# Reading K, V and wq in 64 KB pieces, each written to two neighbouring partitions

## The chip, the cores and the metric

The kernel runs on one core of one Trainium2 chip. The metric is device time in microseconds (us); lower is better. Times are medians of several runs. Runs of each kernel within 0.3% count as undisturbed ("fast"). Where a ratio of two kernels is given, it is the mean time of the one kernel's fast runs over the mean of the other's fast runs of the same rounds, so it is not quite the ratio of the medians that stand beside it.

## The reference

One decoding step of a transformer layer for a single token: layer norm, grouped-query attention against a cache of 65,536 keys for each of 8 key/value heads, then a gated feed-forward block. Shortened to what matters (not word for word):

```python
def _A_ref(x, k_cache, v_cache, wq, wo):          # x is the normed token
    q = (x @ wq)                                   # 32 heads of 128
    k = jnp.repeat(k_cache, 4, axis=1)             # k_cache, v_cache: (1, 8, 65536, 128) bf16
    v = jnp.repeat(v_cache, 4, axis=1)
    scores = jnp.einsum("bhqd,bhkd->bhqk", q, k) * (Dh ** -0.5)
    p = _softmax(scores, axis=-1)
    o = jnp.einsum("bhqk,bhkd->bhqd", p, v)
    return o.transpose(...).reshape(B, Sq, Hq * Dh) @ wo
```

K and V are 134 MB each. Every byte is used once, so the kernel has to bring 282 MB into the on-chip memory (SBUF, in 128 partitions), and that decides its time: in the profile below the DMA row is at 9 in 39 of 40 slices, while PE, the busiest compute engine, is busy 60% of the span.

## The kernel before

The keys of a head are cut into 4 blocks of 16,384 keys. A block of K or V is 4 MB: partition p takes 128 consecutive keys, which are 32 KB in one piece, in memory and in the partition. Four slots of 32 KB a partition form a ring; a load waits until the slot's last user is done. All large loads are issued by SP (SyncE), in the order wq, K0 to K3, then K and V in turn.

```python
SLOT = T * DH                                  # 128 keys x 128: 32 KB a partition
ring = sb("ring", [128, NSLOT * SLOT], bf16)   # NSLOT = 4
...
order = [("wq", 0)]
order += [("K", b) for b in range(NR)]
for b in range(NR, NB):
    order += [("K", b), ("V", b - NR)]
order += [("V", NB - 4), ("V", NB - 3), ("V", NB - 2), ("V", NB - 1), ("wg", 0), ("wu", 0), ("wd", 0)]
...
        if k == "wq":
            dma("sp", lambda e, d=dst: e.dma_start(d.rearrange("p (k n) -> p k n", k=4),
                A_wq.rearrange("(p k) n -> p k n", p=128)), f"r{s}", deps, "wq")
...
            src = cache[0, h, r * BLK:(r + 1) * BLK, :].rearrange("(p t) d -> p (t d)", t=T)
            if ld == ("V", NB - 1):
                ...                            # the last V block goes in two parts
            else:
                dma("sp", lambda e, d=dst, sr=src: e.dma_start(d, sr), f"r{s}", deps, f"{k}{b}")
```

For each K block the vector engine (DVE) transposes 8 chunks, the matrix engine (PE) makes the scores, and four blocks later PE multiplies with V. ACT and POOL in the profiles are the scalar engine and GpSimd.

Of the kernel before, what the change touches and what calls it, by code (L numbers as in the profile page):

```python
# [9 lines left out]
ALU = mybir.AluOpType  # L10
# [12 lines left out]
NSLOT = 4  # L23
# [3 lines left out]
WH = 4 * WJ  # L27
PO_BANKS = (5, 6)
MISC = 7


class Prog:
# [10 lines left out]
    def op(self, eng, fn, deps=(), name=None):  # L43
        assert name is None or name not in self.where, name
        self.ops[eng].append(dict(fn=fn, deps=[d for d in deps if d], name=name, dma=None))
        if name:
            self.where[name] = (eng, len(self.ops[eng]) - 1)

    def dma(self, eng, fn, sem, deps=(), name=None):
        self.op(eng, fn, deps, name)  # L50
        rec = self.dma_sems.setdefault(sem, dict(sem=None, count=0))
        rec["count"] += 16
        self.ops[eng][-1]["dma"] = (sem, rec["count"])
# [43 lines left out]
def bass_sequential_preLN__gqa_block_cached__glu_gated_glu__decode_kernel(  # L97
# [10 lines left out]
    SLOT = T * DH  # L108
# [7 lines left out]
    with ExitStack() as es:  # L116
        def sb(name, shape, dt):
            return es.enter_context(nc.sbuf_tensor(name, shape, dt))

        ring = sb("ring", [128, NSLOT * SLOT], bf16)  # L120
# [52 lines left out]
        def ps(bank, c0, c1, p0=0, p1=128):  # L173
            return PS[p0:p1, bank * 512 + c0: bank * 512 + c1]

        def psap(bank, c0, dims, p0=0, np_=128):
            return bass.AP(tensor=PS, offset=p0 * 4096 + bank * 512 + c0, ap=[[4096, np_]] + dims)

        def slot_ap(s):
            return ring[:, s * SLOT:(s + 1) * SLOT]  # L180

        P = Prog(nc, es)
        op, dma = P.op, P.dma
# [12 lines left out]
        def freed(ld):  # L196
            if ld is None:
                return None
            k, b = ld
            return {"wq": "q", "K": f"T{b}.{NC - 1}", "V": f"PV{b}"}[k]  # L200

        dma("act", lambda e: e.dma_start(x_row[:, :], A_x[0]), "x", name="x")
        V_SPLIT = [(0, 6), (6, 8)]
        for ld in order:
            k, b = ld
            s = slot_of[ld]
            dst = slot_ap(s)
            deps = [freed(prev[ld])]
            if k == "wq":
                dma("sp", lambda e, d=dst: e.dma_start(d.rearrange("p (k n) -> p k n", k=4),  # L210
                    A_wq.rearrange("(p k) n -> p k n", p=128)), f"r{s}", deps, "wq")
            elif k in ("wg", "wu"):
                w = B_w_gate if k == "wg" else B_w_up
                dma("sp", lambda e, d=dst, w=w: e.dma_start(d[:, 0:4 * FF].rearrange("p (k n) -> p k n", k=4),
                    w.rearrange("(p k) n -> p k n", p=128)), f"r{s}", deps, k)
            elif k == "wd":
                src = B_w_down.rearrange("(p r) n -> p r n", p=128)
                for i, (r0, r1) in enumerate(WD_SPLIT):
                    dma("sp", lambda e, d2=dst[:, r0 * D:r1 * D].rearrange("p (r n) -> p r n", n=D), sr=src[:, r0:r1, :]:
                        e.dma_start(d2, sr), f"wd{i}", deps if i == 0 else (), f"wd{i}")  # L220
            else:
                h, r = b // NR, b % NR
                cache = A_k_cache if k == "K" else A_v_cache
                src = cache[0, h, r * BLK:(r + 1) * BLK, :].rearrange("(p t) d -> p (t d)", t=T)
                if ld == ("V", NB - 1):
                    for i, (c0, c1) in enumerate(V_SPLIT):
                        dma("sp", lambda e, d=dst, sr=src, a=c0 * CH, z=c1 * CH: e.dma_start(d[:, a:z], sr[:, a:z]),
                            f"vl{i}", deps if i == 0 else (), f"V{b}.{i}")
                else:
                    dma("sp", lambda e, d=dst, sr=src: e.dma_start(d, sr), f"r{s}", deps, f"{k}{b}")  # L230
            if ld == ("V", NB - 4):
                for i, (j0, nj, nr) in enumerate(WO):
                    src = A_wo[j0 * DH:(j0 + nj) * DH, :]
                    dst = ktw[:, j0 * D:(j0 + nj) * D]
                    if nr:
                        src = src.rearrange("(p r) n -> p (r n)", r=nr)
                    else:
                        src, dst = src.rearrange("(j p) n -> p j n", p=128), dst.rearrange("p (j n) -> p j n", j=nj)
                    dma("sp", lambda e, src=src, dst=dst: e.dma_start(dst, src), f"wo{i}",  # L239
                        [f"S{NB - 1}"] if i == 0 else (), f"wo{i}")  # L240
# [26 lines left out]
        def ln_stats(i, src_dep, bank, c0):  # L267

            op("dve", lambda e: e.tensor_copy(hT[i][:, :], ps(*src_dep[1])), [src_dep[0]], f"hT.{i}")
            op("dve", lambda e: e.tensor_tensor(sq[:, :], hT[i][:, :], hT[i][:, :], ALU.mult), [f"hT.{i}"], f"sq.{i}")  # L270
            op("dve", lambda e: e.tensor_reduce(st[i][:, 0:1], hT[i][:, :], AX.X, ALU.add), (), f"sta.{i}")
            op("dve", lambda e: e.tensor_reduce(st[i][:, 1:2], sq[:, :], AX.X, ALU.add), [f"sq.{i}"], f"st.{i}")
            op("pe", lambda e: e.matmul(ps(bank, c0, c0 + 2), lhsT=onesf[:, :], rhs=st[i][:, :], start=True, stop=True),
               [f"st.{i}", f"sta.{i}", "onesf"], f"tot.{i}")
# [13 lines left out]
        for kt in range(4):  # L288
            lhsT = bass.AP(tensor=x_row, offset=kt, ap=[[D, 1], [4, 128]])
            op("pe", lambda e, lhsT=lhsT, kt=kt: e.matmul(ps(MISC, kt, kt + 1), lhsT=lhsT, rhs=ident[0:1, 0:1], start=True, stop=True,  # L290
                                                          skip_group_check=True),
               ["x", "ident"] if kt == 0 else (), "xTp" if kt == 3 else None)
        for b in PO_BANKS:
            op("pe", lambda e, b=b: e.matmul(ps(b, 0, 512), lhsT=zrow[0:1, 0:128], rhs=zrow[0:1, :], start=True, stop=True),
               ["zrow"], f"z{b}")
        ln_stats(0, ("xTp", (MISC, 0, 4)), 0, 0)
        op("dve", lambda e: e.tensor_copy(xT[:, :], hT[0][:, :]), ["hT.0"], "xT")
# [17 lines left out]
        for je in range(4):  # L315
            src = qh[:, je * 128:(je + 1) * 128]
# [3 lines left out]
        for i in range(4):  # L320
            dst = bass.AP(tensor=ktw, offset=32 * i * KTW_ROW + W0 + i * 32 + NC - 1,
                          ap=[[KTW_ROW, 32], [WH, HKV], [WJ, 4], [NC, 4]])
            src = psap(2, 0, [[4, HKV], [32, 4], [1, 4]], 32 * i, 32)
# [38 lines left out]
        def softmax(h):  # L362
# [3 lines left out]
               [f"mx{NR * h + r}" for r in range(NR)], f"gm{h}")  # L366
            op("pe", lambda e: e.matmul(ps(MISC, 0, 128, 0, 1), lhsT=gm[:, k:k + 1], rhs=identf[:, :], start=True, stop=True),  # L367
               [f"gm{h}", "identf", "xT", f"ls{h - 1}" if h else None], f"gmT{h}")
            op("dve", lambda e: e.tensor_reduce(gmj[:, 4 * k:4 * k + 4], ps(MISC, 0, 128, 0, 1).rearrange("p (i a c) -> p a i c", a=4, c=NC),
                                                AX.XY, ALU.max), [f"gmT{h}"], f"gmj{h}")  # L370
            op("dve", lambda e: e.tensor_copy(gmrep[:, :].rearrange("p (i a c) -> p i a c", a=4, c=NC),  # L371
                                              bass.AP(tensor=gmj, offset=4 * k, ap=[[8, 1], [0, 4], [1, 4], [0, NC]])),
               [f"gmj{h}"], f"gmrep{h}")
            op("pe", lambda e: e.matmul(ps(MISC, 128, 129), lhsT=gmrep[0:1, :], rhs=one_f[0:1, 0:1], start=True, stop=True),  # L374
               [f"gmrep{h}", "onef"], f"neg{h}")
            op("act", lambda e: e.activation(negmax[:, k:k + 1], ps(MISC, 128, 129), AF.Copy, scale=-att_scale),  # L376
               [f"neg{h}", f"E{NR * h - 5}" if h >= 2 else None], f"negmax{h}")
# [115 lines left out]
        for i, (nm, bank) in enumerate((("wg", GB), ("wu", UB))):  # L493
# [7 lines left out]
            if i == 0:  # L501
                for g in range(4):
                    for kt in range(4):
                        dst = psap(YB, kt, [[4, 32]], 32 * g, 1)
                        op("pe", lambda e, g=g, kt=kt, dst=dst: e.matmul(
                            dst, lhsT=hT[1][:, kt:kt + 1], rhs=identf[:, 32 * g:32 * g + 32],
# [53 lines left out]
```

## Time and profile before

| | before |
|---|---|
| time, median of 4 runs | 667.54 us (667.23 to 667.81) |
| bytes from memory | 282.33 MB |
| PE, DVE, ACT busy | 60%, 54%, 5% |
| first data packet begins | 1.76 us after the first instruction |
| last load has landed | 662.5 us |

The head of the page of before: busy times, then the span in 40 slices. In the DMA row a 9 means that the 16 DMA engines were at least 90% busy in that slice; GB/s is what they moved.

```profile
span 665.9 us, 5728 instructions
## 1 busy us (share of the span) xinstructions
PE 396.3 (60%) x2545; PEld 162.8 (24%) x2545; DVE 359.2 (54%) x408; ACT 34.1 (5%) x90; POOL 8.5 (1%) x12
...
DMA  9999999999999999999999999999999999999996
GB/s 378 440 433 417 439 436 425 428 439 428 423 440 433 423 435 433 430 427 438 429 427 436 430 430 429 432 433 429 435 425 436 429 426 439 430 429 409 427 426 249
DMA packets 11586, 282.70 MB, mean 425 GB/s; under 512 B 1193, under 2 KB 2218, under 8 KB 2602
```

```profile
start us, us, engine line op out<-in xcount [idle before <-releaser]
0.74 0.39 SPq L210 DMA_DIRECT2D ring<-in_A_wq_dram  x1
```

### The profile page before, as it was taken

What the parts mean: (1) busy time and instruction counts of PE and PEld (TensorE: products, weight loads), DVE (VectorE), ACT (ScalarE), POOL (GpSimd) and SP (SyncE); (2) the same over time, 40 slices, a digit from 0 to 9 for tenths busy, and PEclk for the clock granted to TensorE, in tenths of its full rate; (3) what the DMA queues carried; (4) which work ended last, traced back from release to release, by engine and by line L of the source; (5) the groups of instructions that cost most, each with busy time, mean ns of one, the idle gap of its engine ahead of it and who ended that gap; (6) DMA issues with size and microseconds to landing.
All of it is one profiled execution on the core that took longest, in us unless ns stands there. A gap on an engine that the chain in (4) does not pass through costs nothing.

```text
span 665.9 us, 5728 instructions
## 1 busy us (share of the span) xinstructions
PE 396.3 (60%) x2545; PEld 162.8 (24%) x2545; DVE 359.2 (54%) x408; ACT 34.1 (5%) x90; POOL 8.5 (1%) x12
## 2 busy tenths in 40 slices
PE   3778586565458664555665644666554567655344
PEld 2522232222123221222222212222221222223212
DVE  6579865574447655464555744476544645553002
ACT  0200100020002000020000200010000200002000
POOL 4000000000000000000000000000000000000000
PEclk9789798677787866788876778887677987768566
DMA  9999999999999999999999999999999999999996
GB/s 378 440 433 417 439 436 425 428 439 428 423 440 433 423 435 433 430 427 438 429 427 436 430 430 429 432 433 429 435 425 436 429 426 439 430 429 409 427 426 249
DMA packets 11586, 282.70 MB, mean 425 GB/s; under 512 B 1193, under 2 KB 2218, under 8 KB 2602
## 3 DMA queue, kind: packets, MB, share of 16 engines
q1 hardware_dynamic: 11560, 282.33, 98.9%
q8 instruction: 20, 0.33, 0.2%
q14 instruction: 4, 0.03, 0.0%
q10 hardware_dynamic: 2, 0.00, 0.0%
HBM read 282.33 MB, written 0.00 MB: 424 GB/s over the span
## 4 chain that ended last, share of the span: by engine, by line
DMA 67%; DVE 22%; PE 9%; ACT 1%; issue 0%; SPq 0%
DMA ring<-in_A_k_cache_dram 58%; DVE ktw L342 21%; PE PS L356 6%; DMA ring<-in_A_v_cache_dram 4%; DMA ring<-in_B_w_up_dram 4%; DMA ring<-in_A_wq_dram 2%; PE PS L307 1%; PE PS L419 1%; DVE M_sb L343 1%; ACT ktw L324 0%; DVE PT_sb L388 0%; PE PS L521 0%; PE PS L497 0%; SPq L239 0%; DVE hh L513 0%
## 5 line engine op out<-in xcount | busy, mean ns | idle before, releaser
L356 PE MATMUL PS<-ktw 128*128 128x512 bf16 x1024 | 294.1, 449 | 201.3 <-DVE ktw L342 196.1
L342 DVE STREAM_TRANSPOSE ktw<-ring 128x1024 f32<-128x1024 f32 x256 | 292.1, 1207 | 180.9 <-DMA ring<-in_A_k_cache_dram 180.9
L356 PEld LDWEIGHTS PS<-ktw 128*128 128x128 bf16 x1024 | 107.4, 110 | 384.6 <-DVE ktw L342 243.7
L419 PE MATMUL PS<-ring,PT_sb 128*16 128x512 bf16 x1024 | 70.6, 424 | 21.1 <-DMA ring<-in_A_v_cache_dram 21.1
L343 DVE TENSOR_REDUCE M_sb<-PS 128x1 f32<-128x512 f32 x32 | 22.1, 692 | 49.9 <-PE PS L356 49.9
L419 PEld LDWEIGHTS PS<-ring,PT_sb 128*16 128x16 bf16 x1024 | 28.4, 113 | 53.8 <-DMA ring<-in_A_v_cache_dram 25.3
L376 ACT ACTIVATE negmax<-PS 128x1 f32<-128x1 f32 x8 | 1.4, 171 | 550.2 <-PE PS L374 550.2
L388 DVE STREAM_TRANSPOSE PT_sb<-P_sb 128x512 bf16<-128x512 bf16 x32 | 21.8, 711 | 11.9 <-ACT P_sb L385 11.9
L433 DVE CAST O<-PS 128x4 bf16<-128x4 f32 x8 | 1.3, 162 | 39.1 <-PE PS L430 39.1
L385 ACT ACTIVATE P_sb<-PS,negmax 128x512 bf16<-128x512 f32 x32 | 21.6, 685 | 0.3
L307 PE MATMUL PS<-ring,xz 128*32 128x128 bf16 x128 | 9.7, 253 | 3.0 <-DMA ring<-in_A_wq_dram 3.0
L307 PEld LDWEIGHTS PS<-ring,xz 128*32 128x32 bf16 x128 | 9.6, 116 | 3.0 <-issue 3.0
L284 POOL TENSOR_TENSOR rstd<-ve,nhalf 128x1 f32<-128x1 f32 x2 | 1.1, 554 | 645.6 <-DVE ve L282 645.6
L430 PE MATMUL PS<-sel_bf,po_sb 128*128 128x4 bf16 x32 | 2.0, 168 | 11.4 <-ACT po_sb L427 11.4
L427 ACT ACTIVATE po_sb<-PS,rl 128x512 bf16<-128x512 f32 x8 | 5.5, 693 | 45.1 <-PE PS L419 45.1
L367 PE MATMUL PS<-identf,gm 128*1 128x128 f32 x16 | 3.0, 271 | 7.8 <-DVE gm L365 7.8
L385 ACT ACTIVATION_READ_ACCUMULATOR P_sb<-PS,negmax 128x1 f32 x32 | 6.5, 202 | 0.0
L456 PE MATMUL PS<-O,ktw 128*128 128x1 bf16 x128 | 4.9, 173 | 2.6 <-DMA ktw<-in_A_wo_dram 2.4
L257 DVE TENSOR_SCALAR rows_i<-rows_i 128x128 int32<-128x128 int32 x1 | 6.1, 6101 | 0.0
L259 DVE TENSOR_SCALAR cols_i<-cols_i 128x128 int32<-128x128 int32 x1 | 6.0, 6028 | 0.0
L374 PE MATMUL PS<-one_f,gmrep 1*128 1x1 f32 x16 | 3.0, 256 | 4.9 <-DVE gmrep L371 4.9
L456 PEld LDWEIGHTS PS<-O,ktw 128*128 128x128 bf16 x128 | 4.6, 118 | 2.9 <-DMA ktw<-in_A_wo_dram 2.2
(72 smaller groups left out, 56.8 us busy)
## 6 DMA issues: line engine op xcount, KB each, us to landing
ring<-in_A_k_cache_dram SPq DMA_DIRECT2D x32, 4096.0 KB, 29.7
ring<-in_A_v_cache_dram SPq DMA_DIRECT2D x31, 4096.0 KB, 35.6
ring<-in_A_wq_dram SPq DMA_DIRECT2D x1, 4096.0 KB, 12.1
ring<-in_A_v_cache_dram SPq DMA_DIRECT2D x1, 3072.0 KB, 32.6
ktw<-in_A_wo_dram SPq DMA_DIRECT2D x1, 2048.0 KB, 14.7
ktw<-in_A_wo_dram SPq DMA_DIRECT2D x2, 1024.0 KB, 18.1
ring<-in_B_w_gate_dram SPq DMA_DIRECT2D x1, 1792.0 KB, 38.5
ring<-in_B_w_up_dram SPq DMA_DIRECT2D x1, 1792.0 KB, 24.6
```

Of the source, the lines that this page charges most:

```text
L257: op("dve", lambda e: e.tensor_scalar(rows_i[:, :], rows_i[:, :], 3, 3, op0=ALU.arith_shift_right, op1=ALU.bitwise_and), ["rows"], "rows2")
L259: op("dve", lambda e: e.tensor_scalar(cols_i[:, :], cols_i[:, :], 3, None, op0=ALU.bitwise_and), ["cols"], "cols2")
L307: op("pe", lambda e, kt=kt, n=n, last=last: e.matmul(ps(1, 0, 128, 0, 32), lhsT=xz[:, kt * 63 + 31 - n: kt * 63 + 63 - n], rhs=wq_v[:, kt, ...
L342: op("dve", lambda e, d=dst, sr=src: e.transpose(d, sr), deps, f"T{b}.{c}")
L343: op("dve", lambda e: e.tensor_reduce(M_sb[:, b % 8:b % 8 + 1], ps(b % NS, 0, 512), AX.X, ALU.max), [f"S{b}"], f"mx{b}")
L356: op("pe", lambda e, n=n, je=je, c=c: e.matmul(ps(b % NS, 0, 512), lhsT=w_ap(h, je, c), rhs=kt_ap(n, je), start=(c == 0 and je == 0), stop ...
L367: op("pe", lambda e: e.matmul(ps(MISC, 0, 128, 0, 1), lhsT=gm[:, k:k + 1], rhs=identf[:, :], start=True, stop=True), [f"gm{h}", "identf", ...
L385: op("act", lambda e, b=b: e.activation(P_sb[:, (b % 4) * 512:(b % 4 + 1) * 512], ps(b % NS, 0, 512), AF.Exp, bias=negmax[:, k:k + 1], sca ...
L388: op("dve", lambda e, b=b: e.transpose(PT_sb[:, (b % 8) * 512:(b % 8 + 1) * 512], P_sb[:, (b % 4) * 512:(b % 4 + 1) * 512]), [f"E{b}", f"P ...
L419: op("pe", lambda e, lhsT=lhsT, tq=tq, t0=t0, c=c: e.matmul(ps(bank, 0, 512, 32 * tq, 32 * tq + 16), lhsT=lhsT, rhs=ring[:, s * SLOT + t0 ...
L427: op("act", lambda e: e.activation(po_sb[:, :], ps(PO_BANKS[k], 0, 512), AF.Copy, scale=rl[:, k:k + 1]), [f"PV{NR * h + NR - 1}", f"rl{h}" ...
L456: op("pe", lambda e, lhsT=lhsT, r=r, nt=nt, end=end: e.matmul(ps(YT, nt, nt + 1), lhsT=lhsT, rhs=src[:, r:r + 1], start=False, stop=end, s ...
```

## The change

The intent: the reads are twice as long and half as many, so whatever each read costs besides its bytes is paid half as often. Two neighbouring partitions hold 64 KB that lie together in memory, so one read can feed both. For this the changed kernel adds the copy as a bare instruction with 64 source rows of 64 KB and a separate destination pattern (partition step 1 twice, then step 2, 64 times).

```diff
+SB_PART = 1 << 18
...
+        def load_wide(e, col, src, n, w):
+            row = NSLOT * SLOT
+            wide = bass.AP(tensor=src.tensor, offset=src.offset, ap=[[w * n, 128 // w], [1, w * n]])
+            return e.add_instruction(mybir.InstDMACopy(
+                name=nc.get_next_instruction_name(), engine=mybir.EngineType.SP, queue="qSPDynamicHW", mode="Copy",
+                cce_op=ALU.bypass, ins=e.lower_ap_dma(wide), outs=e.lower_ap_dma(ring[:, col:col + n]),
+                dst_dge_shape=(SB_PART, w, w * SB_PART, 128 // w, 0, 1, 0, 1),
+                bass_dst_dge_shape=((w * row, 128 // w), (row, w), (1, n))))
...
-                dma("sp", lambda e, d=dst: e.dma_start(d.rearrange("p (k n) -> p k n", k=4),
-                    A_wq.rearrange("(p k) n -> p k n", p=128)), f"r{s}", deps, "wq")
+                dma("sp", lambda e, s=s: load_wide(e, s * SLOT, A_wq, SLOT, 2), f"r{s}", deps, "wq")
...
-                    dma("sp", lambda e, d=dst, sr=src: e.dma_start(d, sr), f"r{s}", deps, f"{k}{b}")
+                    dma("sp", lambda e, s=s, sr=src: load_wide(e, s * SLOT, sr, SLOT, 2), f"r{s}", deps, f"{k}{b}")
```

The last V block, wo and the feed-forward weights are loaded as before.

## The prediction

> **What bounds it now.** The page's slice table has the DMA row at 9 (90% or more) in 39 of 40 slices, nearly all at 423 to 440 GB/s, while PE is 60% busy, DVE 54%, ACT 5%. Taking the trace's packet records one by one, all 16 DMA engines have a packet in flight without a gap from about 12.7 us to the last weight landing at about 658 us. The chain of waits agrees: from 95 to 589 us it only alternates between K landings (57.6% of the span) and the DVE transposes that they release. So the span is (bytes / DMA rate) plus about 20 us, before the data flows and after the last landing, that the change does not touch.
>
> **The packets.** In the records a packet takes almost exactly bytes / 27.2 GB/s plus a constant: 7,168 B takes 272 ns (263.5 + 8.5), 16,384 B 611 to 615, 32,768 B 1213 at the 5th percentile, 1216 at the median, 1220 in the mean (1204.7 + 8 to 15). 16 x 27.2 is 435 GB/s[...]. So 32 KB packets already run at 432 of 435 GB/s.
>
> **What the change does.** Bytes, destinations, order of issue, semaphores and waits stay; 64 loads (wq, 32 K, 31 V) change from 128 rows of 32 KB to 64 rows of 64 KB with two writes each. Per DMA engine that is 512 reads now and 256 then. If the constant (8.5 ns) is paid per read, 256 x 8.5 = 2.2 us go; if the stalls above it (15 ns in the mean) halve as well, 3.9 us; if it is paid per write, nothing. All of it is on the critical path, because the stream is continuous. The bound, no cost per packet at all, is 512 x 15 = 7.7 us (1.2%), so a gain over 2% is practically excluded.
>
> **The danger** is which engine writes which partition. [...] The diff does not tell how rows are dealt out; I give this a little less than one chance in four.
>
> **Prediction.** 665.9 us (667.7 less 1.8), 80% range 663.3 to 671. Faster by over 2%: 0.03; within 2%: 0.75; slower: 0.22.
>
> **What would show each step.** About 7,500 packets in all instead of 11,586, the 64 KB ones of about 2418 ns (2409.4 + 8.5); if the records stay 32 KB of 1213 ns, the constant belongs to the write and the gain is nil. The DMA row stays 9; issue to landing about 29.6 us for K. DVE and PE busy times unchanged, the first landing (wq, 12.1 us) within 0.2 us.
>
> **What would make it wrong.** [...] 64 KB packets clearly over 2.5 us, or uneven between engines, and under 400 GB/s per slice; then K landings lengthen and everything follows. [...] Or a gain over 4 us, which would mean that part of the 1204.7 ns itself is no rate limit.

The 27.2 GB/s in the prediction is the slope of the packet records of before: 32,768 B take 1213 ns and 7,168 B take 272 ns, so 941 ns for 25,600 B; about 8.5 ns of either packet are left over, and 435 GB/s is 16 times that slope. The sum came to 667.7 - 1.8 = 665.9 us. The "slower: 0.22" and the upper end of the range are the author's guess.

## More of the kernel before

No compute engine is busy for more than 60% of the span (PE); the DMA engines are 90% busy or more in every slice but the last. The stretch from 100 to 590 us shows it without the ends (after the stretch: its length, busy time of each engine, granted clock, DMA share, GB/s):

```profile
core 0: us, PE busy (x) PEld busy (x) DVE busy (x) ACT busy (x) POOL busy (x), PEclk, DMA share, GB/s
100.00:590.00 490.00, 288.39 (x1660) 113.57 (x1660) 269.03 (x286) 21.44 (x60) 0.00 (x0) 0.78 1.00 431
```

The share is 1.00: a packet is in flight on every DMA engine all the time.

The issue of the loads, by tile on the SP queue (duration in ns: least, median, most), and the first load in the timeline:

```profile
L230 SPq DMA_DIRECT2D ring<-in_A_k_cache_dram x32: 327/328/530, 1.2 to 559.4; - x32
...
L210 SPq DMA_DIRECT2D ring<-in_A_wq_dram x1: 392/392/392, 0.7 to 0.7; - x1
```

## The result, and the profile after

| | before | after |
|---|---|---|
| time, median of 4 runs | 667.54 us (667.23 to 667.81) | 667.88 us (667.68 to 668.07) |
| ratio of fast runs | | 1.0006 (95%: 0.9992 to 1.0021) |
| first data packet begins | 1.76 us | 2.35 us |
| wq landed after its issue began | 12.14 us | 12.75 us |
| last load has landed | 662.5 us | 662.9 us |

The time is the same within the noise. The head of the page of after:

```profile
span 665.8 us, 5792 instructions
## 1 busy us (share of the span) xinstructions
PE 395.1 (59%) x2545; PEld 162.1 (24%) x2545; DVE 359.3 (54%) x408; ACT 34.2 (5%) x90; POOL 8.5 (1%) x12
...
DMA  9999999999999999999999999999999999999996
GB/s 378 438 441 435 409 422 441 430 437 434 441 414 429 437 419 437 438 441 422 429 425 427 441 434 429 422 437 431 433 441 422 425 422 437 438 441 399 422 416 267
DMA packets 7491, 282.70 MB, mean 425 GB/s; under 512 B 1193, under 2 KB 2218, under 8 KB 2602
```

There are 4095 packets fewer, so the reads really were merged; the mean rate is still 425 GB/s. (The single slices swing more because a packet's bytes are counted in the slice where it starts.) The stretch 100 to 590 us of after:

```profile
core 0: us, PE busy (x) PEld busy (x) DVE busy (x) ACT busy (x) POOL busy (x), PEclk, DMA share, GB/s
100.00:590.00 490.00, 287.50 (x1660) 113.05 (x1660) 268.45 (x286) 21.44 (x60) 0.00 (x0) 0.78 1.00 432
```

431 and 432 are too coarse to tell 0.3% apart, so two finer readings of the trace are used from here on.

*Landings.* Each load's landing is in the trace, as the semaphore updates of its 16 engines. From one load to the fourth next, in the same slot, the quiet gaps are 38.85 us in both kernels: 9.71 us a block of 4 MB.

*Lost time.* At a moment t, take t less (bytes moved by then / 431.85 GB/s), the bytes from the packet records (those that bring in data; 0.33 MB of instruction packets are left out); 431.85 is simply 4 MB (4,194,304 bytes) / 9.7125 us, a round reference pace. If two kernels keep the same distance in lost time, their streams run at one pace; if one gains, the distance shrinks.

| lost time, us | at 6 us | at 50 us | at 300 us | at 590 us |
|---|---|---|---|---|
| before | 2.53 | 2.48 | 3.22 | 4.08 |
| after | 3.13 | 3.07 | 3.81 | 4.67 |
| after less before | 0.60 | 0.59 | 0.59 | 0.59 |

So the wide reads gave back nothing in 584 us of streaming, and 0.6 us were lost once, before the first packet. On the SP queue of after:

```profile
L207 SPq MOVE_SHAPE ring<-in_A_k_cache_dram x32: 24/24/382, 1.6 to 560.0; - x32
L207 SPq DMA_DIRECT2D ring<-in_A_k_cache_dram x32: 615/616/627, 2.0 to 560.0; - x32
...
L207 SPq DMA_DIRECT2D ring<-in_A_wq_dram x1: 774/774/774, 0.8 to 0.8; - x1
```

```profile
start us, us, engine line op out<-in xcount [idle before <-releaser]
0.80 0.77 SPq L207 DMA_DIRECT2D ring<-in_A_wq_dram  x1
```

Every wide load has one more instruction (the destination pattern is moved into place, 24 ns; 64 loads, and 5792 - 5728 = 64 instructions more) and its issue takes 616 ns in place of 328. In the stream this is hidden (the difference in lost time stays 0.59 us), because other loads are queued: in the median a K load of after lands 29.7 us after its issue, and a block passes in 9.71 us. For wq, the first load, it is not hidden: its issue takes 774 ns in place of 392, and from the end of the issue to the first data packet it is 0.78 us in place of 0.63.

The theories to be told apart:
- **Theory 1**: the constant of about 9.4 ns a packet (9712.5 ns for a block / 8 packets an engine = 1214.1 ns, less 32,768 B / 27.2 GB/s = 1204.7 ns) belongs to the written piece (still 32 KB), so the stream gains nothing; the wide wq load starts 0.6 us late and that is all.
- **Theory 0**, the one behind the prediction: the constant belongs to the read; a gain of about 1 to 2 us exists and was eaten by the late start.
- **Theory 2**: all 16 engines together run into a ceiling of 431.9 GB/s, whatever the pieces.

### The profile page after: what moved, and what is told of

Read it like the earlier page. It is cut to its first block, busy times and chain, and to the rows that moved or that the text cites. A ratio compares the mean times of both kernels' runs of the same rounds, so it can differ in the third digit from the quotient of the medians.

```text
span 665.8 us, 5792 instructions
## 1 busy us (share of the span) xinstructions
PE 395.1 (59%) x2545; PEld 162.1 (24%) x2545; DVE 359.3 (54%) x408; ACT 34.2 (5%) x90; POOL 8.5 (1%) x12
## 4 chain that ended last, share of the span: by engine, by line
DMA 69%; DVE 23%; PE 6%; ACT 1%; issue 0%; SPq 0%
DMA ring<-in_A_k_cache_dram 56%; DVE ktw L352 22%; DMA ring<-in_A_v_cache_dram 8%; PE PS L366 3%; DMA ring<-in_B_w_down_dram 3%; DMA ring<-in_A_wq_dram 2%; PE PS L317 1%; PE PS L429 1%; ACT ktw L334 0%; DVE M_sb L353 0%; DVE PT_sb L398 0%; PE PS L531 0%; PE PS L456 0%; ACT P_sb L395 0%; SPq L207 0%
## 6 DMA issues: line engine op xcount, KB each, us to landing
ring<-in_A_k_cache_dram SPq DMA_DIRECT2D x32, 32.0 KB, 29.7
```

## The experiments

Nine kernels ran with profiles. Three more never ran.

### e1_wq_plain: K and V wide, wq as before

```diff
-                dma("sp", lambda e, s=s: load_wide(e, s * SLOT, A_wq, SLOT, 2), f"r{s}", deps, "wq")
+                dma("sp", lambda e, d=dst: e.dma_start(d.rearrange("p (k n) -> p k n", k=4),
+                    A_wq.rearrange("(p k) n -> p k n", p=128)), f"r{s}", deps, "wq")
```

> K and V in 64 KB reads as in the change, wq back to 32 KB reads. Theory 1 (the constant of about 9.4 ns belongs to the write, so the stream gains nothing, and the 0.65 us by which every landing is late come only from the first load, wq): wq lands 12.1 us after its issue again, all later landings are where they were before, 9.71 us apart, and the time is that of before within 0.2 us (667.3 to 667.7). Theory 0 (the prediction: the constant belongs to the read, and 0.9 to 2.2 us of gain were eaten by the late start): 665.3 to 666.8. If the late start comes from every wide load, not the first: as the change, 667.9.

Measured: correct, 667.26 us against 667.34 (5 and 9 runs), ratio 1.0001 (0.9987 to 1.0014). The first data packet begins at 1.76 us again. Lost time is 2.48 at 50 us and 4.05 at 590 us, that of before (2.48, 4.08) within 0.03 us. wq took 12.36 us to land in place of the expected 12.1: the last of its 16 engines came in a little later, with the same bytes moved in total. **The late start comes from the first load, and in the profiled runs 63 wide loads of K and V gain at most 0.03 us in the stream.** The interval of the time alone would still allow a gain of 0.9 us. The traces, one execution of each kernel, speak against it: from 50 to 590 us the four kernels with plain K and V (before, e2, e4, p_wait_x) lost 1.56 to 1.61 us, the two with wide ones (e1 and the changed kernel) 1.56 and 1.58.

### e2_wq_only: only wq wide

The opposite edit: in the changed kernel the K and V line is put back.

> Only wq in 64 KB reads, K and V as before. Theory 1: wq lands 0.65 us later than before (12.75 us after issue), everything after it is late by the same, and the time is that of the change, 667.8 to 668.2 or so. Theory 0: slower than the change by the gain that K and V bring, 668.5 to 670.

Measured: correct, 668.51 us against 667.34, ratio 1.0018 (1.0005 to 1.0030). By its time alone this run falls into theory 0's range, not theory 1's. Its trace speaks for theory 1: the first packet begins at 2.38 us, and lost time is 3.07 at 50 us and 4.65 at 590 us, the changed kernel's values (3.07, 4.67) with none of its wide K and V loads. The rest of the difference arises after 590 us: in all, the last load landed 0.93 us later than in e1, of which 0.6 us is stream. A landing is counted at the last of the 16 engines' updates, and the spread of the 16 at the last full K and V landings was 3.6 us here and 3.4 us in e1 and in the changed kernel, which covers about half of that rest. (In the kernel before the spread was 0.5 us at the first load and 3.5 us at these; in s_r32w32, below, where nothing is computed, it stayed at 0.6 us. Why it grows was not shown.) The intervals of this ratio and of the changed kernel's (0.9992 to 1.0021) overlap; whether the remaining half microsecond is real stays open.

### e4_wq_raw: plain 32 KB reads, wq added as a bare instruction

```diff
-                dma("sp", lambda e, d=dst: e.dma_start(d.rearrange("p (k n) -> p k n", k=4),
-                    A_wq.rearrange("(p k) n -> p k n", p=128)), f"r{s}", deps, "wq")
+                dma("sp", lambda e, s=s: e.add_instruction(mybir.InstDMACopy(
+                    name=nc.get_next_instruction_name(), engine=mybir.EngineType.SP, queue="qSPDynamicHW", mode="Copy",
+                    cce_op=ALU.bypass, ins=e.lower_ap_dma(bass.AP(tensor=A_wq.tensor, offset=A_wq.offset, ap=[[SLOT, 128], [1, SLOT]])),
+                    outs=e.lower_ap_dma(slot_ap(s)))), f"r{s}", deps, "wq")
```

The wide loads are bare instructions too. The first branch of the expectation is that the late start comes with the bare instruction as such; the second, that it comes with the destination pattern.

> All loads as before with 32 KB reads, but the wq load is added as a bare instruction, as the wide one is, [...] without the extra destination pattern. [...] issue of wq takes clearly more than 0.39 us and wq lands late, up to 12.75 us after issue, time about 667.9. If it comes from the destination pattern that has to be loaded for the two-partition write: issue 0.39 us, landing 12.1 us, time of before.

Measured: correct, 667.86 us against 667.34, ratio 1.0007 (0.9994 to 1.0019). The issue of wq in the timeline of this run, to be held against 0.39 us before and 0.77 us after:

```profile
0.74 0.60 SPq L210 DMA_DIRECT2D ring<-in_A_wq_dram  x1
```

The first packet begins at 2.11 us, 0.35 us later than before; lost time at 590 us is 4.43, also 0.35 more. So neither branch of the expectation holds alone: of the 0.6 us, 0.35 come with the bare instruction and the remaining 0.25 with the wide copy and its destination pattern. What makes a bare instruction slower to issue (597 ns in place of 392) was not shown.

### p_wait_x: before, with the first load made late on purpose

```diff
-                    A_wq.rearrange("(p k) n -> p k n", p=128)), f"r{s}", deps, "wq")
+                    A_wq.rearrange("(p k) n -> p k n", p=128)), f"r{s}", deps + ["x"], "wq")
```

> The kernel before, all loads plain, but the first load (wq) waits until the small row x has landed, so that the stream starts late by a known amount (the wait gives about 1 to 2 us; the trace tells). If a late start is paid in full at the end, as theory 1 says of the change's 0.6 us: the time is above before by what the first data packet is late, within 0.4 us, and the lost time stays constant from 6 us to the end of K and V. If the stream or the tail takes it up: less than half of it shows in the time.

Measured: correct, 668.46 us against 667.23, ratio 1.0020 (1.0006 to 1.0034). In its timeline the first load is issued 1.25 us later:

```profile
1.99 0.39 SPq L210 DMA_DIRECT2D ring<-in_A_wq_dram  x1
```

The first packet begins at 3.02 us, 1.26 us later than before; lost time is 1.25 us more at 50 us and 1.22 more at 590 us; the median time is 1.23 us more (95% interval of the ratio: 0.4 to 2.3 us). **The late start of the stream was paid in full to the end of K and V, and by the medians in the time too**; the DMA row of this run has a 9 in all 38 slices between its first (8) and its last (6).

### s_r32w32, s_r64w32, s_r64w64: the loads alone

A kernel that loads the 64 blocks of K and V into the ring and computes nothing. Its output is wrong, which doesn't matter for the time. The core of it, with the source as `(p t) d -> p (t d)` and the three ways to load:

```python
src = cache[0, h, r * blk:(r + 1) * blk, :].rearrange("(p t) d -> p (t d)", p=128)
s = i % NSL
P.dma("sp", lambda e, s=s, src=src: load(e, s * SLOT, src, SLOT), f"r{s}", [f"l{i - NSL}"] if i >= NSL else (), f"l{i}")
# r32w32: 4 slots of 32 KB, plain; r64w32: 4 slots of 32 KB, load_wide with w = 2
# r64w64: 2 slots of 64 KB, plain, so 32 loads of 8 MB
```

> Loads alone, wrong result on purpose: the 64 blocks of K and V (268.4 MB), 4 MB each, reads of 32 KB written as 32 KB, no compute and no wait but for the ring slot. All theories: landings 9.71 us apart, as in the kernel before; 64 x 9.71 = 622 us and some us at the ends.

> The same with reads of 64 KB written as two of 32 KB. Theory 1 (constant per write): landings 9.71 us apart, same as s_r32w32 within 0.01 us. Theory 0 (constant per read): 9.68 us, 2.2 us less in all. Theory 2 (a ceiling of 431.9 GB/s for all engines together): 9.71 us.

> The same bytes in 32 loads of 8 MB, 64 KB read and 64 KB written to one partition each. Theory 1: 8 x (2409.4 + 9.4) = 19.35 us between landings, against 19.42 us for two loads of s_r32w32, 2.4 us less in all. Theory 0: the same 19.35 us, but then s_r64w32 has it too. Theory 2 (ceiling): 19.42 us, as the others.

Measured (2 runs each; the gap is the mean over loads 2 to 15 of a slot, for the same 4 MB):

| loads alone | read | written | time | gap for 4 MB | ns a read | over its bytes / 27.2 GB/s |
|---|---|---|---|---|---|---|
| s_r32w32 | 32 KB | 32 KB | 628.65 us | 9.713 us | 1214 | 9.4 |
| s_r64w32 | 64 KB | 2 x 32 KB | 629.05 us | 9.715 us | 2429 | 19.4 |
| s_r64w64 | 64 KB | 64 KB | 626.28 us | 9.680 us | 2420 | 10.5 |

(A gap of 9.713 us is 8 reads of 32 KB on each engine, so 1214 ns a read; one of 9.715 us is 4 reads of 64 KB.) With two pieces written a read costs about twice the constant, with one piece written about once, at the same read length. (The mean of s_r64w64 holds a few disturbed landings near 100 us and before; its quiet gaps, 38.70 us for 16 MB, give 9.4 in place of 10.5.) s_r64w64 is 2.37 us faster than s_r32w32, where 2.4 were expected. The stretch 100 to 590 us of s_r32w32, s_r64w32 and s_r64w64, in this order (nothing computes; the last three columns are clock, DMA share and GB/s):

```profile
100.00:590.00 490.00, 0.00 (x0) 1.00 1.00 431
100.00:590.00 490.00, 0.00 (x0) 1.00 1.00 432
100.00:590.00 490.00, 0.00 (x0) 1.00 1.00 433
```

The line of packets on the page of s_r32w32, of s_r64w32 and of s_r64w64:

```profile
DMA packets 9218, 268.44 MB, mean 428 GB/s; under 512 B 1025, under 2 KB 1026, under 8 KB 1026
```

```profile
DMA packets 5123, 268.45 MB, mean 428 GB/s; under 512 B 1025, under 2 KB 1026, under 8 KB 1026
```

```profile
DMA packets 4610, 268.44 MB, mean 430 GB/s; under 512 B 513, under 2 KB 514, under 8 KB 514
```

The first has 8192 packets of 32 KB, the other two 4096 of 64 KB each; the rest are small. The last two have the same reads and a different pace. **Theory 0 falls with s_r64w32, theory 2 with s_r64w64**: 431.9 GB/s is no ceiling, for 4 MB in 9.68 us are 433. s_r64w32 also starts late (first packet at 2.33 us against 1.75) and is 0.40 us slower.

One rival these times do not exclude: in all these runs an engine writes 8 pieces a load, so a cost of about 75 ns for each *load* would fit as well (s_r64w64 has 32 loads fewer and saves 2.37 us; e5, below, has 186 more and takes 14.14 us more). The packet records decide. They do not name the engine, but a packet can be joined to the one that starts where it ends. Followed so from 100 to 560 us, the packets *inside* a load start 1213.2 ns apart in s_r32w32, 2426.2 in s_r64w32 and 2417.3 in s_r64w64 (means over 472, 689 and 258 loads of an engine); the end of a load adds only 6 to 8 ns. So a second written piece costs about 9 ns inside a load too, and halving the reads changes nothing (2426.2 against twice 1213.2). Of the 9.4 ns a piece, a little under 1 ns is the end of the load.

### e5_r8_w8: K and V in 8 KB pieces

On the kernel before (so wq plain too): each block in four ordinary loads of 1 MB, the keys dealt out as `(c p t) d -> c p (t d)` with c = 4, K and V alike; the last block of each stays as it was.

```diff
+        def load_wide(e, col, src, n, w):
+
+            return e.dma_start(ring[:, col:col + n], src)
...
+                        q = SLOT // 4
+                        flat = cache[0, h, r * BLK:(r + 1) * BLK, :].rearrange("(c p t) d -> c p (t d)", c=4, p=128)
+                        for c in range(4):
+                            dma("sp", lambda e, c=c, s=s, sr=flat[c]: load_wide(e, s * SLOT + c * q, sr, q, 1), f"r{s}",
+                                deps if c == 0 else (), f"{k}{b}" if c == 3 else f"{k}{b}.{c}")
```

(Here load_wide is only a name: it makes an ordinary load.)

> wq plain; every K and V block (but the last of each) in 4 loads of 1 MB, 128 reads of 8 KB written as 8 KB. Control for e6. Constant of 9.4 ns a packet, read or write: 3 more packets for each 32 KB, 28 ns more for each 32 KB, 9.94 us for each block of 4 MB in place of 9.71, about 14 us more in all: 681 to 683. A ceiling by bytes alone (theory 2): no more than 668.5.

Measured: correct, 681.43 us against 667.29 (ratio 1.0211). The stretch 100 to 590 us of this run falls from 431 to 422 GB/s with the same full DMA share:

```profile
100.00:590.00 490.00, 283.58 (x1611) 111.07 (x1612) 265.63 (x283) 21.44 (x60) 0.00 (x0) 0.77 1.01 422
```

14.14 us over 62 blocks are 228 ns a block; each engine handles 24 pieces more for a block, so 9.5 ns a piece (about 8.7 if the ends of 3 more loads, 6 to 8 ns each, are taken off). So the constant is about the same at 8, 32 and 64 KB (9.5, 9.4, and 9.4 to 10.5 ns in s_r64w64). In these runs it does not grow with the bytes.

### e3_far_pairs: each 64 KB read to partitions p and p+64

```diff
-                dst_dge_shape=(SB_PART, w, w * SB_PART, 128 // w, 0, 1, 0, 1),
-                bass_dst_dge_shape=((w * row, 128 // w), (row, w), (1, n))))
+                dst_dge_shape=(64 * SB_PART, w, SB_PART, 128 // w, 0, 1, 0, 1),
+                bass_dst_dge_shape=((row, 128 // w), (64 * row, w), (1, n))))
```

> As e1_wq_plain, but each 64 KB read of K and V is written to partitions p and p+64 in place of two neighbours (the last K block and the last V block plain; K and V are permuted alike, so the result stays right). Every DMA engine then writes to two halves of the partitions. If it matters which partitions an engine writes [...]: packets of 64 KB take clearly more than 2432 ns, up to twice that, landings are 10 to 19 us apart and the time is 700 to 1250 us[...]. If it does not matter, 667.3 to 667.9, and the danger in the prediction did not exist.

(The factor of up to two in it, and the ranges that follow from it, are the author's guess; no earlier run showed one.)

Measured: correct, 1095.36 us in the fast run, which is the profiled one. (A second run took 1151.95 us and counts as slow; the median of both, 1123.65, mixes the two.) Slices and stretch of the profiled run:

```profile
DMA  9999999999999999999999999999999999999986
GB/s 305 228 202 228 228 231 230 230 231 247 236 233 231 242 233 231 230 230 231 230 240 237 237 243 233 257 319 341 362 329 360 346 370 348 280 253 205 216 230 251
```

```profile
100.00:590.00 490.00, 179.27 (x900) 64.59 (x900) 152.61 (x166) 13.88 (x39) 0.00 (x0) 0.66 1.01 233
```

The DMA row is as full as ever while the rate is halved: the row shows packets in flight, not bytes moved. A 64 KB packet took 4.44 us in the median (nine in ten took 2.86 to 4.70) in place of 2.43. So which partitions a read is written to matters greatly here (1095 us against 667), as the prediction feared, and the changed kernel does not run into it: with neighbouring partitions, its packets keep 2.43 us. Nothing else differs from e1, but for one plain K block. By what mechanism the far pairs are slow was not shown, and they are not equally slow throughout: from about 710 to 930 us the rate rises to 319 to 370 GB/s with the same kind of destinations.

### e6_r64_w8, e7_r4_w32 and the changed kernel once more: REFUSED

e6 was e5 with 16 reads of 64 KB for each 1 MB, each written as 8 KB to 8 partitions; e7 had 1024 reads of 4 KB, written as 32 KB; the third, c_after_again, was the changed kernel unchanged, to settle the half microsecond left open under e2. The check before the chip refused all three, since it no longer lets a kernel set the destination pattern by hand; e1, e2, e3 and s_r64w32 had run before that. What was expected:

> The same loads, but each as 16 reads of 64 KB, every one written as 8 KB to 8 neighbouring partitions. Theory 1 (constant per write): as e5, 681 to 683. Theory 0 (constant per read): half the reads of before, 665 to 668. If read and write each bear half of it: 673 to 675.

> wq plain; K and V blocks as 1024 reads of 4 KB written as 32 KB to one partition each (if the chip takes it so; the result tells). If only writes bear the constant: 667.5 or so. If the side with more pieces sets the pace: 7 more packets for each 32 KB, 66 ns more, about 34 us more: 700. If it is not done as meant, the result is wrong and the run says nothing.

> The changed kernel itself once more, because the kernel with only wq in wide reads came out 1.17 us above before and the changed kernel 0.34 us, though both traces show the stream 0.6 us late. If the 0.6 us late start is all (theory 1): 0.4 to 1.1 us above before here too, and the lost time at the first loads 0.6 us more than before's. If wide K and V do give something back (theory 0): within 0.3 us of before.

So it stays open whether reads have a cost of their own when they are shorter than the pieces written. What is shown is the case where reads are as long as the written pieces, or twice as long.

## Why the prediction was right or wrong

- **The range and the class held**: 667.88 us lies in 663.3 to 671, and "within 2%" came true. That is no proof of the mechanism: the range is 7.7 us wide for a gain of 1.8, and both would have held with or without the gain. That the stream is continuous and has hardly any reserve (9.4 of 1214 ns a packet) was right, and it is why nothing large could come of it.
- **The gain of 1.8 us did not come.** The step that failed is "if the constant (8.5 ns) is paid per read, 256 x 8.5 = 2.2 us go". The prediction named the other case, "if it is paid per write, nothing", and weighed it too low. Measured: nothing, 0.59 us of lost time between the two kernels at 50 us and still 0.59 at 590 us. s_r64w32 and s_r64w64 show why: about twice the constant for two written pieces, once for one.
- **The sign that was to tell was badly chosen.** "Records stay 32 KB of 1213 ns" was to mean the constant is the write's, and 64 KB records of 2418 ns that it is the read's. The records became 64 KB and took 2432 ns in the median, which is neither. A packet's record also runs about 4 ns into the next one: in s_r32w32, 8 records of 1218 ns are 9745 ns, but their block passes in 9713. The mean of the records therefore fell by 3.7 ns for each 64 KB (1218.1 twice, against 2432.5) with no change of pace. The gap between landings is the pace; the duration of records is not.
- **"The first landing within 0.2 us" failed**: 12.75 us after issue in place of 12.14. The prediction counted bytes and waits and forgot that another kind of load is issued by other instructions. 24 + 774 ns in place of 392 on the SP queue, and a first packet 0.6 us later, are the whole effect of the change on the stream that the traces show. e1 takes it away, e2 brings it alone, p_wait_x shows that such lateness is paid about one for one.
- **The danger** (which engine writes which partition) was weighed at a little under one in four. e3 shows that a bad choice of partitions is costly, at 1095 us in place of 667; the change as written does not meet it. Which rows each engine got is not recorded in the trace. Only the pace tells the two choices apart (2.43 us a packet for neighbouring pairs, 4.44 for far ones); the prediction's reason for the danger was not shown.

No version tried beats the kernel before. The one thing that gained, writing 64 KB pieces, needs 64 KB of one partition filled by one load, so 8 MB loads across 128 partitions; with the ring's 128 KB a partition that leaves two slots. A block's 8 transposes take DVE about 9.7 us (1207 ns each), so a pair of K blocks would hold its slot at least another 19.3 us after landing. The estimate is that this costs more than the 2.4 us to be had; it was not run.

## What to carry to other kernels

When a DMA stream is full, ask which side of the copy pays the cost a packet has besides its bytes: here it was the written piece, so longer reads into the same pieces gained nothing (629.05 us against 628.65 for the loads alone), and only longer written pieces did (626.28 us). Check a change of a few ns a packet by the distance between landings or by lost time against bytes, not by packet durations, and look at the first load by itself, since a late start of a full stream was paid one for one here (1.26 us late at the first packet, 1.23 us in the time). A full DMA row says that packets are in flight, not that bytes move: at 1095 us it looked as full as at 667. And when two designs differ in pieces and in loads at once, look inside a load before naming what costs.
